# Scores of two steps behind the values, and PSUM banks handed out by hand, in top-k attention with a tanh-shrink feed-forward

## The chip, the cores and the metric

The kernel runs on one core of one Trainium2 chip. The metric is device microseconds (us), the median of the runs shown. A core has TensorE (PE in the profile; its weight loads are PEld), VectorE (DVE), ScalarE (ACT), GpSimd (POOL) and SyncE (SP, which here issues DMAs). [...]

## What is computed

```python
scores = scale * np.matmul(q, k.transpose(0, 1, 3, 2))          # (8, 8, 576, 576), head_dim 64
kth = np.partition(scores, -32, axis=-1)[..., -32:-31]
scores = np.where(scores >= kth, scores, -1000000000.0)
scores = scores - np.max(scores, axis=-1, keepdims=True)
attn = np.exp(scores)
attn = attn / (np.sum(attn, axis=-1, keepdims=True) + 1e-09)
x = np.matmul(attn, v)                                          # then (B,H,S,D) -> (4608, 512)
h = x @ w_in                                                    # 512 -> 2048
out = (h - np.tanh(h)) @ w_out                                  # 2048 -> 512
```

The two weight matrices come as 64-bit floats and are converted on the chip during the first steps; q, k and v are 32-bit floats.

## The kernel before, in words

The work is cut into 144 **steps**. A step is one tile of 128 query rows for a pair of heads (the two heads stand on partitions 0 to 63 and 64 to 127 of the operands); since 576 is 4 x 128 + 64, there are also remainder steps, which take the last 64 rows of two head pairs. Batch 0 has steps 0 to 17, every later batch 18 more. From batch 1 on, steps come in twos (two query tiles of one head pair), and the second of them is `last`.

A step passes through several stages, each some steps behind the one before. The loop over `n` (from -4 to 144 + LAG) issues, in this order, for its turn `n`:

- the mask of step n-1 (ACT L347, POOL L350) and the search of step n (DVE L297 to L319): the 32 largest scores of each row, in four rounds. Between rounds come small jobs: the reciprocal of step n-2 (DVE L389), its division (ACT L396) and its 32x32 transpose (DVE L427);
- the DMAs that spread the transposed weights over partitions (`spread_keys`, through a DRAM tile, into an `et` buffer);
- a share of the feed-forward work (`deal`);
- `values`, five steps (LAG) after a unit's last step: attention weights times v into a PSUM tile `av` (L492), then copied out by ACT (L512) into `xT`. Before step 45 (NEAR) this stands at the head of the turn instead;
- `scores(n+1)`: matmuls into the PSUM tile `scps` (L267), copied out by one ACT instruction (L275). DVE reads half of the scores from PSUM directly;
- the exponentials of step n-1 (ACT L370), more shares of `deal`, and loads (`todo`).

In batch 0 (`pe`) the transposes run on TensorE instead (L464, copied by ACT L467), with `values` two steps behind.

**The feed-forward part** works on units of 256 rows (or 128 for remainders). Its items are lists of matmuls: `ffn_h` fills a PSUM bank of 512 columns in two items (L543), after which ACT takes tanh (L555) and a copy (L556) out of it and POOL subtracts; `ffn_o` accumulates 16 matmuls of 512 columns in one bank (L564, in eight items), which ACT copies out (L574) for the store. How many items each `deal` issues is worked out from the stock and the due times of the units, so TensorE's order is fixed when the program is built.

[...] Each buffer of a pool is a tile of its own, and a new use of it waits for the readers of the old one. Every engine works its instructions in the order of issue; waits between engines are put in by the framework, which follows reads and writes of tiles.

Of the kernel before, what the change touches and what calls it, by code (L numbers as in the profile page):

```python
# [8 lines left out]
AF = mybir.ActivationFunctionType  # L9
# [11 lines left out]
LAG = 5  # L21

NEAR = 45


class Step:
# [25 lines left out]
def kernel(  # L52
# [47 lines left out]
    gpool = pool("g", 4)  # L100
    dpool = pool("d", 2, space=bass.MemoryType.DRAM)
    sc_ps = pool("sc_ps", 1, space=PS)
    zt_ps = pool("zt_ps", 2, space=PS)
    h_ps = pool("h_ps", 2, space=PS)

    ident = consts.tile([P, P], FP32, name="ident")
    make_identity(nc, ident[:])
# [32 lines left out]
    def convert(piece, slot):  # L140


        j, i = piece // CD, piece % CD
        if j < WJ:
            src, dst = moe_w_in[i * P : (i + 1) * P, j * NW : (j + 1) * NW], w_in[j][:, i, :]
        else:
            r0 = ((j - WJ) * FJ + i) * P
            src, dst = moe_w_out[r0 : r0 + P, :], w_out[j - WJ][:, i, :]
        raw, shifted, _ = slot
        nc.sync.dma_start(flat(raw), src.bitcast(U32))  # L150
        nc.sync.dma_start(
            flat(shifted).bitcast(U8)[:, 0 : 8 * NW - 4], src.bitcast(U8)[:, 3 : 8 * NW - 1]
        )
        yield
        hi = raw[:, :, 1]
        f = thpool.tile([P, NW], FP32, tag="th", name="f")
        fu = f[:].bitcast(U32)

        nc.vector.tensor_scalar(fu, hi, 20, 0x7FF, ALU.logical_shift_right, ALU.bitwise_and)  # L159

        e = h_ps.tile([P, NW], FP32, tag="h", name="e")[:] if j < WJ else f[:]
        nc.scalar.activation(e.bitcast(I32), fu, AF.Relu, bias=e896[:], scale=2.0**23)

        nc.vector.tensor_scalar(
            dst.bitcast(U32), shifted[:, :, 0], 0x0FFFFFFF, None, ALU.bitwise_and
        )
        nc.scalar.activation(dst, dst.bitcast(U32), AF.Copy, bias=1.0, scale=2.0**-28)
        yield

        nc.vector.scalar_tensor_tensor(  # L170
            out=fu, in0=hi, scalar=0x80000000, in1=e.bitcast(U32), op0=ALU.bitwise_and, op1=ALU.bitwise_or
        )
        nc.gpsimd.tensor_tensor(dst, dst, f[:], ALU.mult)
        yield
# [9 lines left out]
    def half(t):  # L184
        return slice(t * D, (t + 1) * D)
# [45 lines left out]
    def turn_rows(name, b, hp):  # L231

        d = kqpool.tile([P, S], FP32, tag=f"{name}T", name=f"{name}T")
        {"k": kT, "q": qT}[name][b, hp] = d
        x = raw.pop((name, b, hp))
        if not (b == 0 and hp and turned_pe[0]):
            nc.vector.transpose(d[:], x)  # L237
            return
        for c0, c1, w in ((0, J, P), (J, J + 1, R)):
            zt = zt_ps.tile([P, 512], FP32, tag="zt", name="zt")  # L240
            for c in range(c0, c1):
                o = (c - c0) * P
                nc.tensor.transpose(zt[:, o : o + w], x[0:w, c * P : (c + 1) * P], ident[0:w, 0:w])
            w = (c1 - c0 - 1) * P + w
            nc.scalar.copy(d[:, c0 * P : c0 * P + w], zt[:, 0:w])
# [9 lines left out]
    W2, W4 = S2 // NL, S4 // NL  # L255
    rest = consts.tile([P, 2, S4 + Q], FP32, name="rest")

    def scores(n):
        g = steps[n]
        ps = sc_ps.tile([P, 2, 2, 512], FP32, tag="sc", name="scps")  # L260
        for s in range(2):
            ks = slice(s * S2, (s + 1) * S2)
            for i in range(2 if g.rem else 1):
                qs = slice(JP, S) if g.rem else slice(g.qt * P, (g.qt + 1) * P)
                rows = half(i) if g.rem else slice(0, P)
                for t in range(2):
                    nc.tensor.matmul(  # L267
                        ps[rows, t, s, 0:S2],
                        qT[g.b, g.hp + i][half(t), qs],
                        kT[g.b, g.hp + i][half(t), ks],  # L270
                        start=True,
                        stop=True,
                    )
        sc = scpool.tile([P, 2, 2, S2], FP32, tag="sc", name="sc")
        nc.scalar.copy(sc[:], ps[:, :, :, 0:S2])  # L275
        st[n] = dict(sc=sc, ps=ps)

    def search(n, exact, between):

# [2 lines left out]


        x = st[n]
        sc, ps = x["sc"], x.pop("ps")
        m = x["m"] = mpool.tile([P, 2, TOP], FP32, tag="m", name="m")
        rounds = TOP // 8
        if exact:
# [3 lines left out]
            left = seen[1:]  # L292
        else:
            top = x["top"] = tpool.tile([P, 2, S4 + Q], FP32, tag="top", name="top")
            near, far = ps[:, :, 0, 0:S2], sc[:, :, 1, :]
            a, b = half_max, ps[:, :, 0, S2 : S2 + S4]
            nc.vector.tensor_tensor(b, near[:, :, S4:], far[:, :, S4:], ALU.max)  # L297
            nc.vector.tensor_tensor(a, near[:, :, 0:S4], far[:, :, 0:S4], ALU.max)  # L298

# [149 lines left out]
    def turn_pe(n):  # L449

        g, z = steps[n], st.pop(n)["z"]
        if g.rem:
            et = et_rem
        elif g.i:
            et = ets.pop(n - 1)
        else:
            et = et2[0]
        ets[n] = et
        et = tiles(et, g.nq)[:, :, :, g.i, :].rearrange("p a k j -> p k a j")
        for k0 in range(0, KC, J):  # L460
            kn = min(J, KC - k0)
            zt = zt_ps.tile([P, 512], FP32, tag="zt", name="zt")
            for k in range(kn):
                nc.tensor.transpose(  # L464
                    zt[:, k * P : (k + 1) * P], z[:, (k0 + k) * P : (k0 + k + 1) * P], ident[:]
                )
            nc.scalar.copy(  # L467
                et[:, k0 : k0 + kn],
                zt[:, 0 : kn * P].rearrange("p (k a j) -> p k a j", a=NG, j=G),
            )  # L470
            if k0:
                yield
# [2 lines left out]

        return x.rearrange("p (a i j) -> p i a j", a=NG, i=nq)

    def values(n):


        g = steps[n]
        nq, u = g.nq, g.unit
        et = tiles(ets.pop(n), nq)
        w = nq * P
        av = zt_ps.tile([P, 2, N], FP32, tag="zt", name="av")
        for i in range(2 if g.rem else 1):
            cols = half(i) if g.rem else slice(0, w)
            es = et[:, 2 * i : 2 * i + 2] if g.rem else et
# [1 line left out]
            for c in range(J + 1):  # L490
                for t in range(2):
# [4 lines left out]
                        start=(c == 0),  # L496
                        stop=(c == J),
                    )
        if g.pe:
            rx = rxs.pop(n)  # L500
            for i in range(nq):
# [31 lines left out]
    def ffn_h(u, item):  # L533
# [3 lines left out]
        for f in range(item * per, (item + 1) * per):  # L537
            j, fo = f // FJ, (f % FJ) * P
            s = f * w % 512
            if s == 0:  # L540
                cur[u] = h_ps.tile([P, 512], FP32, tag="h", name="hps")
            for c in range(CD):
                nc.tensor.matmul(  # L543
                    cur[u][:, s : s + w],
# [5 lines left out]
        if item % 2:  # L550
            th = thpool.tile([P, 512], FP32, tag="th", name="th")
            if item % 4 == 1:
                u.g.append(gpool.tile([P, 2, 512], FP32, tag="g", name="g"))
            g = u.g[-1][:, item % 4 // 2, :]
            nc.scalar.activation(th[:], cur[u][:], AF.Tanh)  # L555
            nc.scalar.copy(g, cur[u][:])  # L556
            nc.gpsimd.tensor_tensor(g, g, th[:], ALU.subtract)  # L557

    def ffn_o(u, i, part):
        if part == 0:  # L560
            cur[u] = h_ps.tile([P, DM], FP32, tag="h", name="ops")
        for f in range(2 * part, 2 * part + 2):
            o = f * u.n + i * P
            nc.tensor.matmul(  # L564
                cur[u][:],
                u.g[o // 1024][:, o % 1024 // 512, o % 512 : o % 512 + P],
                w_out[f // FJ][:, f % FJ, :],
                start=(f == 0),
# [2 lines left out]
        if part < CF // 2 - 1:  # L571
            return
        ot = thpool.tile([P, DM], FP32, tag="th", name="ot")
        nc.scalar.copy(ot[:], cur[u][:])  # L574
        for rows, dst in u.blocks[i]:
            nc.sync.dma_start(dst, ot[rows, :])

# [49 lines left out]
    def run(exact):  # L627
# [10 lines left out]
        for i, (b, hp) in enumerate(pairs):  # L638
            n = next(n for n, g in enumerate(steps) if (g.b, g.hp) == (b, hp))
            for x, name in enumerate("kq"):  # L640
                m = max(n - 5 + x, turned.get(name, -4))
                if b == 0 and not exact:
                    m = -4
                at(m, lambda x=(name, b, hp, exact): load_rows(*x))
# [4 lines left out]
                    at_round.setdefault((n - 1, 0), []).append(turn)  # L649
                    turned[name] = n - 1  # L650
                else:
                    at(n - 3 + x, turn)
                    turned[name] = n - 3 + x
            at(n + 1 if b else n - 1, lambda b=b, hp=hp: load_v(b, hp))


# [51 lines left out]


        ready, begun = {}, {}  # L710
        for m, g in enumerate(steps):
            if g.last:
                begun.setdefault(g.unit, m + g.lag)
                if m in done:
                    ready[g.unit] = m + g.lag + g.pe
        before, last = {}, {}
        for u in begun:
            k = 2 if u.tag == "xT" else 1
# [28 lines left out]
                credit -= 1  # L747
            credit = min(credit, 1.0)

        for n in range(-4, NS + LAG):  # L750
            pe = here(-2) and steps[n - 2].pe
            def due():
                for m in (n - LAG, n - LAG + 1, n - LAG + 2):
                    if 0 <= m < NS and steps[m].last and steps[m].lag == n - m:
                        values(m)

            if n < NEAR:
                due()
            share, usable = rate(), converted[0]
            if pe:  # L760
                w = turn_pe(n - 2)
# [11 lines left out]
                spread(n - 2)  # L773
            deal(0.0 if pe else 0.4)
            if n >= NEAR:
                due()
            if here(1):
                scores(n + 1)
            if pe:
                next(w)  # L780
            if here(-1):
# [16 lines left out]

    any_bad = xpool.tile([P, 1], FP32, tag="anybad", name="anybad")
    nc.vector.reduce_max(any_bad[:], bad[:].rearrange("p t n i -> p (t n i)"), axis=mybir.AxisListType.X)  # L800
    cnt = zt_ps.tile([P, 512], FP32, tag="zt", name="cnt")
    nc.tensor.matmul(cnt[0:1, 0:1], any_bad[:], ones[:], start=True, stop=True)
    flag = xpool.tile([1, 1], I32, tag="flag", name="flag")
    nc.vector.tensor_copy(flag[:], cnt[0:1, 0:1])
# [33 lines left out]
```

## Time and profile before

| | |
|---|---|
| runs | 1511.54 us median of 3 (1510.0 to 1512.67) |
| the profiled execution's own time | 1509.65 us |
| its span | 1507.5 us |
| mean granted TensorE clock | 0.982 |
| idle ahead of scores L267 | 18.4 us, of it 8.2 on the first qT, 6.7 on DVE L305 |
| ACT L370, L347, L396 | 288, 288 and 252 instructions of 0.77 us each |
| ACT L512 (values out) | 56 of 0.37 us, 28 of 0.22 us |
| DMA traffic | 221.68 MB, 147 GB/s |

The span is what the profiler saw of the program; the own time of the same execution also holds what lies around it. In a group's line, the columns are: source line, engine, operation, what it writes and reads, shapes, count; then busy time and mean ns of one; then the engine's idle time just before these instructions, and what ended it. A float32 matmul of the code shows as two records. Matmuls are pipelined, so a record's duration is longer than the distance to the next record; the distance is the price.

### The profile page before, as it was taken

Reading aid. Unit: us, or ns where it says so; the run is one execution under the profiler, and the core shown is the slowest. Engines: PE = TensorE matmul, PEld = TensorE weight load, DVE = VectorE, ACT = ScalarE, POOL = GpSimd, SP = SyncE. Lnnn points to the kernel's source line nnn. Section 1 sums busy time; section 2 is a strip of 40 time slices with the busy share of each in tenths; the row PEclk is TensorE's granted clock in tenths of the full one; section 3 lists DMA queues with packets and bytes.
Section 4 is the critical chain, followed back from the end, with each engine's and each line's share of the span. In section 5 each row is a group of like instructions: output and inputs, shape, how many; then the busy total and the mean of one; then the engine's idle time right before and its main releaser. Section 6 shows DMA issues by size and latency. Waiting matters only on the chain.

```text
span 1507.5 us, 25020 instructions
## 1 busy us (share of the span) xinstructions
PE 1426.5 (95%) x7332; PEld 908.2 (60%) x7332; DVE 1295.2 (86%) x4886; ACT 1004.9 (67%) x1813; POOL 879.1 (58%) x1370
## 2 busy tenths in 40 slices
PE   4667898999999999999999999999999999999998
PEld 2454656465666565656565665657575675656673
DVE  7999899999998999999989999899988989886100
ACT  4766777777776777777676676768676676766220
POOL 3777667566565575657565575747474664646120
PEclk9888999999999999999999999999999999999999
DMA  9954123657854685567655865466554766443400
GB/s 277 373 170 167 25 43 92 171 156 153 205 147 140 164 166 156 134 176 171 162 136 146 175 147 165 138 166 159 156 145 117 174 144 177 111 140 105 109 7 17
DMA packets 248563, 221.68 MB, mean 147 GB/s; under 512 B 190816, under 2 KB 197984, under 8 KB 241248
## 3 DMA queue, kind: packets, MB, share of 16 engines
q1 hardware_dynamic: 246640, 219.75, 56.0%
q8 instruction: 61, 1.00, 0.3%
q14 instruction: 86, 0.70, 0.2%
q10 hardware_dynamic: 1776, 0.22, 0.1%
HBM read 136.17 MB, written 83.76 MB: 146 GB/s over the span
## 4 chain that ended last, share of the span: by engine, by line
PE 74%; DVE 15%; ACT 4%; POOL 2%; DMA 2%; issue 1%; SPq 0%; ACTq 0%; DVEq 0%; POOLq 0%
PE ops L564 28%; PE hps L543 28%; PE av L492 9%; PE scps L267 8%; DVE m L316 3%; DVE top L309 2%; DVE rest L319 2%; DVE zx L427 2%; DVE ab L303 1%; DMA w_in<-in_k_dram 1%; DVE f L170 1%; PE zt L464 1%; DVE f L159 1%; DVE top L319 1%; DVE ab L298 1%
## 5 line engine op out<-in xcount | busy, mean ns | idle before, releaser
L564 PE MATMUL ops<-w_out,g 128*128 128x512 f32 x1152 | 517.5, 600 | 2.4 <-POOL bad L354 1.5
L543 PE MATMUL hps<-xT,w_in 128*128 128x256 f32 (+1 forms) x2176 | 466.7, 372 | 1.0 <-ACT g L556 0.9
L350 POOL TENSOR_TENSOR z<-sc,z 128x576 f32<-128x576 f32 x288 | 404.5, 1426 | 86.2 <-ACT z L347 86.2
L543 PEld LDWEIGHTS hps<-xT,w_in 128*128 128x128 f32 x2176 | 392.0, 192 | 75.8 <-issue 21.6
L564 PEld LDWEIGHTS ops<-w_out,g 128*128 128x128 f32 x1152 | 213.3, 191 | 262.3 <-issue 250.3
L347 ACT ACTIVATE z<-sc,tb 128x576 f32<-128x576 f32 x288 | 207.6, 769 | 141.9 <-POOL tb L334 141.2
L557 POOL TENSOR_TENSOR g<-g,th 128x512 f32<-128x512 f32 x144 | 183.6, 1277 | 145.7 <-ACT g L556 140.9
L396 ACT ACTIVATE z<-z,rd 128x576 f32<-128x576 f32 x252 | 180.7, 764 | 97.0 <-DVE rd L389 96.9
L370 ACT ACTIVATE z<-z,nb 128x576 f32<-128x576 f32 x288 | 221.6, 774 | 2.5 <-POOL z L350 2.4
L380 POOL TENSOR_SCALAR rd<-den 128x2 f32<-128x2 f32 x144 | 32.7, 227 | 312.9 <-ACT z L370 307.1
L267 PE MATMUL scps<-kT,qT 64*128 64x288 f32 (+1 forms) x1280 | 189.0, 447 | 18.4 <-DVE qT L237 8.2
L427 DVE STREAM_TRANSPOSE zx<-z 128x1152 f32<-128x1152 f32 x126 | 172.0, 1365 | 35.2 <-ACT z L396 34.6
L309 DVE MAX8 top<-ab 128x8 f32<-128x144 f32 x864 | 194.6, 295 | 0.0
L275 ACT COPY sc<-scps 128x1152 f32<-128x1152 f32 x144 | 160.4, 1114 | 41.8 <-PE scps L267 41.4
L316 DVE MAX8 m<-rest 128x8 f32<-128x168 f32 x576 | 161.6, 322 | 0.0
L267 PEld LDWEIGHTS scps<-kT,qT 64*128 64x128 f32 (+1 forms) x1280 | 102.4, 184 | 94.5 <-issue 19.9
L316 DVE MAX8 m<-top 128x8 f32<-128x144 f32 (+1 forms) x576 | 151.7, 305 | 0.0
L555 ACT ACTIVATE th<-hps 128x512 f32<-128x512 f32 x144 | 84.2, 585 | 64.5 <-PE hps L543 62.1
L303 DVE TENSOR_TENSOR ab<-scps,sc 128x576 f32<-128x576 f32 x144 | 107.6, 748 | 0.0
L297 DVE TENSOR_TENSOR scps<-scps,sc 128x288 f32<-128x288 f32 x144 | 64.6, 449 | 46.1 <-ACT sc L275 45.7
L354 POOL TENSOR_SCALAR bad<-top,tb 128x3 uint8<-128x3 f32 x288 | 95.0, 341 | 0.0
L492 PE MATMUL av<-et,vb 128*64 128x256 f32 (+1 forms) x640 | 76.8, 372 | 18.2 <-ACT et L467 18.2
(78 smaller groups left out, 1536.8 us busy)
## 6 DMA issues: line engine op xcount, KB each, us to landing
there<-zx SPq DMA_DIRECT2D x56, 1152.0 KB, 4.2
spare<-there SPq DMA_DIRECT2D x112, 288.0 KB, 4.7
et<-there SPq DMA_DIRECT2D x112, 288.0 KB, 5.2
kin<-in_k_dram SPq DMA_DIRECT2D x116, 72.0 KB, 2.9
vb<-in_v_dram SPq DMA_DIRECT2D x64, 128.0 KB, 5.9
out_dram<-ot SPq DMA_DIRECT2D x32, 256.0 KB, 3.3
qin<-in_q_dram SPq DMA_DIRECT2D x113, 72.0 KB, 3.7
there<-zx SPq DMA_DIRECT2D x14, 576.0 KB, 5.2
```

Of the source, the lines that this page charges most:

```text
L267: nc.tensor.matmul(ps[rows, t, s, 0:S2], qT[g.b, g.hp + i][half(t), qs], kT[g.b, g.hp + i][half(t), ks], start=True, stop=True,)
L309: nc.vector.max(top[:, t, o : o + 8], low[:, t, i, :])
L316: nc.vector.max(m[:, t, m8], seen[i][t])
L347: nc.scalar.activation(zv[:, t, :], scf[:, t, :], AF.Relu, bias=tb[:, t : t + 1], scale=-BIG)
L350: nc.gpsimd.tensor_tensor(zv[:, t, :], scf[:, t, :], zv[:, t, :], ALU.subtract)
L370: nc.scalar.activation(x["zv"][:, t, :], x["zv"][:, t, :], AF.Exp, bias=x["nb"][:, t : t + 1], scale=scale, accum_out=den[:, t : t + 1],)
L396: nc.scalar.activation(x, x, AF.Copy, scale=rds[n][:, g.i, t : t + 1])
L427: nc.vector.transpose(tiles(zx, g.nq)[:, :, :, g.i, :].rearrange("p c k j -> p k c j"), z[:].rearrange("p (k c j) -> p k c j", c=NG, j=G),)
L492: nc.tensor.matmul(av[half(t), 0, cols], vb[g.b, hp][:, t, c, :] if c < J else vr[g.b, hp][:, t, :], es[:, :, (J + 1) * t + c if c < J els ...
L543: nc.tensor.matmul(cur[u][:, s : s + w], w_in[j][:, c, fo : fo + P], u.xT[:, c, 0:w], start=(c == 0), stop=(c == CD - 1),)
L557: nc.gpsimd.tensor_tensor(g, g, th[:], ALU.subtract)
L564: nc.tensor.matmul(cur[u][:], u.g[o // 1024][:, o % 1024 // 512, o % 512 : o % 512 + P], w_out[f // FJ][:, f % FJ, :], start=(f == 0), sto ...
```

## The change

Four things, with new line numbers in parentheses.

- The pools `zt` and `h` have one buffer each, a tile of two banks (`zts`, `hbs`), and functions `zt_bank()` and `h_bank()` hand out the halves in turn. The feed-forward lines become L591 (for L543), L603, L604 (for L555, L556), L612 (for L564) and L622 (for L574); transposes are L495, their copies L498.
- From step 18 (PAIRS) on, `scores_of_two` makes the scores of steps n+1 and n+2 in one go, at every second turn: the first 320 columns of each head into `scps`, the last 256 into the two `zts` banks (L277), with two ACT copies for each step (L305, L306). The search reads its near half from `scps` as before (L328 to L336).
- `values` (L534, copied out by L560) no longer uses a `zt` buffer, but the half of `hbs` that the feed-forward part did not take last. It may hold two units' values side by side. Its turn is moved to the turns at which scores of two are made, so for every second unit one step later.
- Loads and transposes of k and q come one step earlier.

```diff
+PAIRS = 18
+WIDE = 320
...
-    zt_ps = pool("zt_ps", 2, space=PS)
-    h_ps = pool("h_ps", 2, space=PS)
+    zt_ps = pool("zt_ps", 1, space=PS)
+    h_ps = pool("h_ps", 1, space=PS)
+    zts = zt_ps.tile([P, 2, 512], FP32, name="zts")
+    hbs = h_ps.tile([P, 2, 512], FP32, name="hbs")
+    last_zt, last_hb = [0], [0]
+    def zt_bank():
+        last_zt[0] ^= 1
+        return zts[:, last_zt[0]]
+    def h_bank():
+        last_hb[0] ^= 1
+        return hbs[:, last_hb[0]]
...
+    def scores_of_two(n):
+        ps = sc_ps.tile([P, 2, 2, 512], FP32, tag="sc", name="scps")
+        ends = zts[:].rearrange("p t (i k) -> p i t k", i=2)[:, :, :, 0 : S - WIDE]
+        for i in range(2):
+            products(steps[n + i], lambda rows, t: ps[rows, i, t, 0:WIDE], slice(0, WIDE))
+            products(steps[n + i], lambda rows, t: ends[rows, i, t, :], slice(WIDE, S))
+        for i in range(2):
+            sc = scpool.tile([P, 2, 2, S2], FP32, tag="sc", name="sc")
+            scf = sc[:].rearrange("p t s k -> p t (s k)")
+            nc.scalar.copy(scf[:, :, 0:WIDE], ps[:, i, :, 0:WIDE])
+            nc.scalar.copy(scf[:, :, WIDE:S], ends[:, i])
+            st[n + i] = dict(sc=sc, near=ps[:, i])
...
-            near, far = ps[:, :, 0, 0:S2], sc[:, :, 1, :]
-            a, b = half_max, ps[:, :, 0, S2 : S2 + S4]
+            near, far = ps[:, :, 0:S2], sc[:, :, 1, :]
+            a, b = half_max, ps[:, :, WIDE : WIDE + S4]
...
-            zt = zt_ps.tile([P, 512], FP32, tag="zt", name="zt")
+            zt = zt_bank()
...
-    def values(n):
+    def values(*ns):
+        if steps[ns[0]].pe:
+            bank = zt_bank().rearrange("p (a n) -> p a n", a=2)
+            weigh(ns[0], bank)
+            put_values(ns[0], bank)
+            return
+        bank = hbs[:, last_hb[0] ^ 1].rearrange("p (a n) -> p a n", a=2)
+        for x, n in enumerate(ns):
+            weigh(n, bank[:, x:])
+        for x, n in enumerate(ns):
+            put_values(n, bank[:, x:])
...
-        av = zt_ps.tile([P, 2, N], FP32, tag="zt", name="av")
...
-                cur[u] = h_ps.tile([P, 512], FP32, tag="h", name="hps")
+                cur[u] = h_bank()
...
-            nc.scalar.activation(th[:], cur[u][:], AF.Tanh)
-            nc.scalar.copy(g, cur[u][:])
+            nc.scalar.activation(th[:], cur[u], AF.Tanh)
+            nc.scalar.copy(g, cur[u])
...
-            cur[u] = h_ps.tile([P, DM], FP32, tag="h", name="ops")
+            cur[u] = h_bank()
...
-                m = max(n - 5 + x, turned.get(name, -4))
+                m = max(n - 6 + x, turned.get(name, -4))
...
-                    at(n - 3 + x, turn)
-                    turned[name] = n - 3 + x
+                    at(n - 4 + x, turn)
+                    turned[name] = n - 4 + x
...
             if g.last:
-                begun.setdefault(g.unit, m + g.lag)
+                x = m + g.lag
+                if not g.pe:
+                    x += max(x - PAIRS, 0) % 2
+                    due.setdefault(x, []).append(m)
+                begun.setdefault(g.unit, x)
...
             if n >= NEAR:
-                due()
-            if here(1):
-                scores(n + 1)
+                of_step(n)
+            if here(1) and n + 1 not in st:
+                if n >= PAIRS and here(2):
+                    scores_of_two(n + 1)
+                else:
+                    scores(n + 1)
```

`products` holds the matmuls that stood in `scores`; `weigh` and `put_values` are the two halves of the old `values`, the matmuls and the copies.

More of the change, by code (lines that the diff above doesn't have):

```diff
@@ L159, in convert @@
         nc.vector.tensor_scalar(fu, hi, 20, 0x7FF, ALU.logical_shift_right, ALU.bitwise_and)
-        e = h_ps.tile([P, NW], FP32, tag="h", name="e")[:] if j < WJ else f[:]
+        e = h_bank() if j < WJ else f[:]
         nc.scalar.activation(e.bitcast(I32), fu, AF.Relu, bias=e896[:], scale=2.0**23)
@@ L256, with products @@
     rest = consts.tile([P, 2, S4 + Q], FP32, name="rest")
+    def products(g, out, ks):
+        for i in range(2 if g.rem else 1):
+            qs = slice(JP, S) if g.rem else slice(g.qt * P, (g.qt + 1) * P)
+            rows = half(i) if g.rem else slice(0, P)
+            for t in range(2):
+                nc.tensor.matmul(
+                    out(rows, t),
+                    qT[g.b, g.hp + i][half(t), qs],
+                    kT[g.b, g.hp + i][half(t), ks],
+                    start=True,
+                    stop=True,
+                )
     def scores(n):
-        g = steps[n]
         ps = sc_ps.tile([P, 2, 2, 512], FP32, tag="sc", name="scps")
@@ L262, in scores @@
             ks = slice(s * S2, (s + 1) * S2)
[L263 to L273, printed above, removed]
+            products(steps[n], lambda rows, t: ps[rows, t, s, 0:S2], ks)
         sc = scpool.tile([P, 2, 2, S2], FP32, tag="sc", name="sc")
         nc.scalar.copy(sc[:], ps[:, :, :, 0:S2])
-        st[n] = dict(sc=sc, ps=ps)
+        st[n] = dict(sc=sc, near=ps[:, :, 0, :])
+    def scores_of_two(n):
[10 more added lines that the diff above has]
+            st[n + i] = dict(sc=sc, near=ps[:, i])
     def search(n, exact, between):
         x = st[n]
-        sc, ps = x["sc"], x.pop("ps")
+        sc, ps = x["sc"], x.pop("near")
         m = x["m"] = mpool.tile([P, 2, TOP], FP32, tag="m", name="m")
@@ L461, in turn_pe @@
             kn = min(J, KC - k0)
-            zt = zt_ps.tile([P, 512], FP32, tag="zt", name="zt")
+            zt = zt_bank()
             for k in range(kn):
@@ L476, in in_order, with weigh @@
         return x.rearrange("p (a i j) -> p i a j", a=NG, i=nq)
-    def values(n):
+    def values(*ns):
[9 more added lines that the diff above has]
+            put_values(n, bank[:, x:])
+    def weigh(n, av):
         g = steps[n]
-        nq, u = g.nq, g.unit
+        nq = g.nq
         et = tiles(ets.pop(n), nq)
         w = nq * P
-        av = zt_ps.tile([P, 2, N], FP32, tag="zt", name="av")
         for i in range(2 if g.rem else 1):
@@ L498, in values, with put_values @@
                     )
+    def put_values(n, av):
+        g = steps[n]
+        nq, u = g.nq, g.unit
+        w = nq * P
         if g.pe:
@@ L564, in ffn_o @@
             nc.tensor.matmul(
-                cur[u][:],
+                cur[u],
                 u.g[o // 1024][:, o % 1024 // 512, o % 512 : o % 512 + P],
@@ L573, in ffn_o @@
         ot = thpool.tile([P, DM], FP32, tag="th", name="ot")
-        nc.scalar.copy(ot[:], cur[u][:])
+        nc.scalar.copy(ot[:], cur[u])
         for rows, dst in u.blocks[i]:
@@ L710, in run @@
         ready, begun = {}, {}
+        due = {}
         for m, g in enumerate(steps):
             if g.last:
-                begun.setdefault(g.unit, m + g.lag)
+                x = m + g.lag
[3 more added lines that the diff above has]
+                begun.setdefault(g.unit, x)
                 if m in done:
-                    ready[g.unit] = m + g.lag + g.pe
+                    ready[g.unit] = x + g.pe
         before, last = {}, {}
@@ L748, in deal, with of_step @@
             credit = min(credit, 1.0)
-        for n in range(-4, NS + LAG):
+        def of_step(n):
+            if n in due:
+                values(*due[n])
+        for n in range(-4, NS + LAG + 1):
             pe = here(-2) and steps[n - 2].pe
[L752 to L755, printed above, removed]
             if n < NEAR:
-                due()
+                of_step(n)
             share, usable = rate(), converted[0]
@@ L775, in run @@
             if n >= NEAR:
-                due()
-            if here(1):
-                scores(n + 1)
+                of_step(n)
+            if here(1) and n + 1 not in st:
[3 more added lines that the diff above has]
+                    scores(n + 1)
             if pe:
@@ L800 @@
     nc.vector.reduce_max(any_bad[:], bad[:].rearrange("p t n i -> p (t n i)"), axis=mybir.AxisListType.X)
-    cnt = zt_ps.tile([P, 512], FP32, tag="zt", name="cnt")
+    cnt = zt_bank()
     nc.tensor.matmul(cnt[0:1, 0:1], any_bad[:], ones[:], start=True, stop=True)
```

## The prediction

> **What bounds the kernel now.** I read the page first: engine shares, slices, chain of waits.
>
> ```profile
> span 1507.5 us, 25020 instructions
> ...
> PE 1426.5 (95%) x7332; PEld 908.2 (60%) x7332; DVE 1295.2 (86%) x4886; ACT 1004.9 (67%) x1813; POOL 879.1 (58%) x1370
> ...
> PE   4667898999999999999999999999999999999998
> ...
> PEclk9888999999999999999999999999999999999999
> ...
> PE 74%; DVE 15%; ACT 4%; POOL 2%; DMA 2%; issue 1%; SPq 0%; ACTq 0%; DVEq 0%; POOLq 0%
> ```
>
> TensorE is full from the sixth slice on, and the chain is its own. So the question about every edit is whether a matmul starts later. The groups by line say what it waited for:
>
> ```profile
> L564 PE MATMUL ops<-w_out,g 128*128 128x512 f32 x1152 | 517.5, 600 | 2.4 <-POOL bad L354 1.5
> L543 PE MATMUL hps<-xT,w_in 128*128 128x256 f32 (+1 forms) x2176 | 466.7, 372 | 1.0 <-ACT g L556 0.9
> ...
> L275 ACT COPY sc<-scps 128x1152 f32<-128x1152 f32 x144 | 160.4, 1114 | 41.8 <-PE scps L267 41.4
> ...
> L555 ACT ACTIVATE th<-hps 128x512 f32<-128x512 f32 x144 | 84.2, 585 | 64.5 <-PE hps L543 62.1
> ```
>
> The 144 tanh inputs (L543) and 36 outputs (L564) of the feed-forward part, 180 fillings of a PSUM bank, waited 3.4 us in all. The reason is in the code: a bank is emptied by ACT (tanh L555 and copy L556, or copy L574) while TensorE fills the other. Next, the timeline of TensorE in the middle, then ACT's and TensorE's in the tail, where ACT has little else to do:
>
> ```profile
> 707.69 1.95 PE L492 MATMUL av<-spare,vb 128*64 128x256 f32 x16
> 709.47 0.60 PE L492 MATMUL av<-spare,vr 128*64 128x256 f32 x4
> 710.00 1.24 PE L267 MATMUL scps<-kT,qT 64*128 64x288 f32 x8
> 711.17 7.13 PE L564 MATMUL ops<-w_out,g 128*128 128x512 f32 x16
> 718.24 1.24 PE L267 MATMUL scps<-kT,qT 64*128 64x288 f32 x8
> 719.41 2.84 PE L564 MATMUL ops<-w_out,g 128*128 128x512 f32 x6
> ```
>
> ```profile
> 1445.20 0.37 ACT L512 COPY xT<-av 128x256 f32<-128x256 f32 x1 [1.71 <-PE av L492]
> 1448.87 0.60 ACT L555 ACTIVATE th<-hps 128x512 f32<-128x512 f32 x1 [3.30 <-PE hps L543]
> 1449.37 0.58 ACT L556 COPY g<-hps 128x512 f32<-128x512 f32 x1
> ```
>
> ```profile
> 1445.05 13.22 PE L543 MATMUL hps<-xT,w_in 128*128 128x256 f32 x60
> ```
>
> Two prices come from here. Sixteen records of 512 columns take 7.13 us, 0.446 each, so 0.871 ns a column; 16 records of 256 fill a bank in 3.57 us. The bank begun at 1445.05 is full at 1448.62; its copy ends at 1449.95, 1.33 us later. TensorE does not see this today, being in the other bank.
>
> **Part 1: fewer score visits (a gain).** The eight score records of 710.00 are four pairs side by side: 8 x 288 x 0.871 / 2 = 1.00 us. The visit takes 1.17 (718.24 to 719.41), so entering and leaving cost 0.17. 62 pairs make 62 visits fewer: 62 x 0.17 = 10.5 us, all on TensorE. Bounds: nothing, to 25 us (0.4 a visit, the weight load's idle time at such a change being 0.38 to 0.76). Columns stay the same: 320 + 256 for 288 + 288.
>
> **Part 2: four score copies for two (ACT).** L275 takes 1.11 us for 1152 elements, copies of 512 take 0.58; a step's two parts (640 and 512) I put at 1.2, nearly nothing more. What changes is the lump: in the built program the first copy waits for a matmul of the second step, and DVE's first operation of the first step waits for the second step's first copy. So DVE starts about 4 us after the scores begin instead of 2.75 (710.00 to 712.75). DVE's 17.5 us a pair (1102.9 busy between 200 and 1376 us, 63 pairs) stay under the 18.7 that a pair takes now (the scores of step 18 start at 208 us, those of step 143 at 1376), and the second step's scores lie ready. I cost this at nothing while a pair takes TensorE over 20 us.
>
> **Part 3: the banks as one tile (the loss).** The two feed-forward banks become halves of one tile, hbs. In the built program, every wait named, the matmul that opens one half waits for the last ACT instruction that read the *other*: the one opening columns 512 on waits for the copy out of columns 0 to 511, which waits for the bank's last matmul, just issued. I counted TensorE's work between a filled bank and the matmul that waits for its emptying. Before: never under 3.57 us, hence the idle 1.0 and 2.4. After: none at all in 133 cases of L604 (tanh and copy) and 34 of L622 (output copy), of 180; 8 more have under 2.2 us. The values sit in the same tile and inherit the wait (25 of these cases). The overlap is gone: TensorE stops, ACT empties, TensorE goes on. All 7 us of feed-forward matmuls per step stand behind the waiting one, and the scores behind them.
>
> Price of a wait, lower end: 1.33 + 0.05 (a matmul starts 0.05 us after the ACT instruction that it waited for, as after L467) = 1.38; for the output copy 0.80. Upper end: I paired all L555/L556 with the bank's last matmul. Between 200 and 1376 us, bank end to copy end has a median of 2.42 and a mean of 2.59 us (1.11 when ACT is free), for L574 a mean of 2.04. But that queue stands since ACT there waits for DVE (L347 for tb 141 us, L396 for rd 97 us), and a slower TensorE lets DVE get ahead. So I follow one pair from the start of its scores. Scores done at 2.2, half a bank of feed-forward at 4.0. ACT: four score copies 2.0 to 4.3, exponentials (L370, two of 0.77 and 0.19) to 6.2, tanh and copy to 7.3: a stop of 3.3. In each of the next three banks ACT has two lots of 1.43 or 1.9 us against 3.57 of filling, and is waiting: 1.38 each. Mean 1.85. Where the bank is full before the values (12 pairs) the long stop is missing, about 1.45. I take 1.75, and 1.3 for the output copy.
>
> - Middle: 112 x 1.75 = 196 and 28 x 1.3 = 36.
> - Tail, ACT free: 14 x 1.38 + 5 x 0.80 = 23.
> - Opening (18 steps, 200 us): zts is one tile too, so the second bank of transposes waits for the first's copy, 0.59 and some 0.3 around it: 18 x 0.89 = 16; 13 waits on L554 of some 0.6 = 8; eight feed-forward banks = 11. TensorE is idle for 61 of these 200 us, so part is hidden: 20, bounds 0 and 40.
> - Values emptied behind the scores: the copy is 0.37 against 2.0 of scores; 5 for late ones, bounds 0 and 15.
>
> **Part 4: the clock.** The stretches of the opening show the price of a long stop (columns: time, PE, PEld, DVE, ACT, POOL busy, granted clock, DMA):
>
> ```profile
> 51.80:55.20 3.40, 0.01 (x2) 0.01 (x2) 3.40 (x12) 2.95 (x6) 3.25 (x5) 0.86 1.03 398
> 55.20:60.00 4.80, 3.48 (x17) 2.68 (x19) 4.77 (x18) 2.52 (x7) 3.83 (x8) 0.50 1.08 360
> ```
>
> After 3.4 us idle the clock is halved; the stops under 1.8 us elsewhere left it at 1.00, one of 2.4 us took 3.4 us of half clock. The long stop of 3.3 us comes in some 18 pairs; half of them at 3.4 us lost gives 30, bounds 0 and 70. [...]
>
> **Moved at no cost:** loads and turns of k and q come one step earlier, with the same distance between them and the same DMAs; values of every second unit one step later, still ahead of the reuse of their et buffer.
>
> [...]
>
> **Sum:** 196 + 36 + 23 + 20 + 5 + 30 - 10 = 300. On the profiled execution's 1509.65 us (span 1507.5 and 2.2 around it; the median of the runs is 1.9 higher) that is **1810 us**. All lower ends: 133 x 1.38 + 34 x 0.80 - 25 = 186, so 1696; all upper: 141 x 2.6 + 36 x 2.1 + 40 + 15 + 70 = 567, so 2077.
>
> **Rivals.**
> - *Faster, 1500.* The wait is met when TensorE arrives, and part 1 is left. For: as written, the code alternates the banks as before. It decides if some 1.4 us of other TensorE work lies between a full bank and the next opening; 167 of 180 have none. 6%.
> - *ACT free everywhere, 1700 to 1760.* Stops at their floor, no halved clock. For: DVE gains slack. Against: copies and exponentials stand ahead of the tanh after each pair. 20%.
> - *ACT's queue as it is today, 1880 to 2050.* Stops of 2.6 us, and the clock halved more often, which lengthens the stops' surroundings. For: today's mean. 26%.
> - *Forecast, 1760 to 1880:* 48%.
>
> Range 1700 to 1950: it leaves the first rival and the upper part of the third out. A measurement of this kernel tells 0.2% from no change; faster 0.05, within 0.2% 0.01, slower 0.94: the first rival's 6% and the rest.
>
> **What would show it.** Waits of L591, L612 and L534 on ACT's g and ot: some 170, together 200 to 300 us, in place of 3.4. TensorE's share near 80%, its busy sum near 1430. In the tail a gap of 1.3 to 1.4 us after every 3.57 us. DVE idle some 15% more, waiting on L305. Clock tenths of 9 with some 8s. Wrong if the waits on g are few, or if their mean is under 1.3 or over 2.2; if the clock holds, 30 go; if DVE's wait on L305 leads the chain, part 2 was not free.

## The result and the profile after

The changed kernel takes 1906.91 us (median of 4 runs, 1897.29 to 1912.35) against 1511.99: a ratio of 1.2608, 95% interval 1.2546 to 1.267. The profiled execution took 1901.9 us by its own time, its span is 1900.0.

The page after, first the shares and slices:

```profile
span 1900.0 us, 25054 instructions
...
PE 1505.7 (79%) x7332; PEld 944.6 (50%) x7332; DVE 1295.9 (68%) x4886; ACT 1022.8 (54%) x1937; POOL 878.1 (46%) x1370
...
PE   4667787778778888787878878787978878787887
...
PEclk7578998889999999999999999999999999999999
```

No engine is full any more. TensorE's digits, 9 from the sixth slice on before, are now mostly 7 and 8, and its busy sum rose by 79 us, for the same 7332 records: part of the time it ran at a lower clock (mean granted clock 0.935, before 0.982). What TensorE waited for (columns: engine and line, releaser, us in total, times, longest):

```profile
PE hbs L591 <- ACT g L604: 192.0, 105, 6.7
PE hbs L612 <- ACT ot L622: 28.6, 11, 5.6
PE hbs L534 <- ACT ot L622: 25.6, 13, 6.1
PE hbs L612 <- ACT g L604: 25.4, 16, 2.6
...
PE hbs L534 <- ACT g L604: 19.2, 12, 2.8
PE hbs L591 <- ACT ot L622: 17.9, 10, 4.4
```

These six rows are the wait on the other half of the tile: 167 times, 308.7 us, where the kernel before had 3.4 us. The other engines wait in turn; ACT's and DVE's rows:

```profile
ACT xT L560 <- PE hbs L534: 177.7, 51, 7.4
ACT th L603 <- PE hbs L591: 177.5, 69, 5.6
ACT z L378 <- POOL tb L365: 124.9, 95, 3.1
ACT z L427 <- DVE rd L420: 89.8, 60, 3.8
```

```profile
DVE scps L328 <- ACT sc L305: 250.8, 58, 7.7
DVE zx L458 <- ACT z L427: 134.7, 60, 7.5
```

TensorE and ACT now work by turns, and DVE, which waited 46 us for score copies, waits 251 for those of the pairs. ACT's own waits for DVE's chain (the mask for `tb`, the division L427 for the reciprocal) are only about a tenth smaller than before, when they were:

```profile
ACT z L347 <- POOL tb L334: 141.2, 116, 3.6
ACT z L396 <- DVE rd L389: 96.9, 62, 2.9
```

So DVE got no lead on ACT from a slower TensorE: it gets its scores from TensorE.

The three stages of the span (columns as in the prediction's stretches; the cuts are the scores of step 18 and of step 143):

```profile
0.00:243.50 243.50, 156.27 (x908) 106.71 (x908) 187.66 (x671) 142.38 (x266) 140.09 (x208) 0.77 0.51 160
243.50:1736.40 1492.90, 1214.64 (x5893) 755.92 (x5892) 1095.44 (x4177) 847.33 (x1609) 710.00 (x1130) 0.96 0.47 118
1736.40:1900.00 163.60, 134.77 (x536) 81.94 (x534) 12.80 (x39) 33.08 (x62) 28.02 (x32) 0.99 0.13 38
```

Before, the same stages took 208.3, 1167.4 and 131.8 us; they grew by 35, 325 and 32. The wait in its plain form stands at the end of the middle, where ACT has little else to do:

```profile
1718.87 3.72 PE L591 MATMUL hbs<-xT,w_in 128*128 128x256 f32 x16 [1.16 <-ACT g L604]
1723.76 3.72 PE L591 MATMUL hbs<-xT,w_in 128*128 128x256 f32 x16 [1.16 <-ACT g L604]
```

A bank of 3.57 us now comes every 4.89 us: 1.32 a wait, of which the profile shows 1.16 as idle. The rest counts as busy: the bank's 16 records last 3.72 us, 0.15 longer than the 3.57 after which a next matmul starts when none waits (from here on the drain).

**The account.** Span +392.5 us. TensorE's idle time went from 65.9 to 380.5: +315. By the clock's record TensorE was busy for 187.4 us at half clock, before for 38.7. But the record begins only at 19.6 us, in the kernel before at 50.9, and the profile counts what lies ahead of it as full speed. It was half: up to there the eight score records of a visit take 2.29 us in both kernels, as they do inside the changed kernel's recorded half-clock stretch from 23.0 to 98.1; at full clock they take 1.24 (710.00 in the prediction's timeline). One visit of the kernel before, ahead of its record, and one of the changed kernel, in that stretch:

```profile
47.92 2.29 PE L267 MATMUL scps<-kT,qT 64*128 64x288 f32 x8
```

```profile
26.84 2.29 PE L277 MATMUL scps<-kT,qT 64*128 64x288 f32 x8
```

With the busy time ahead of the record, 8.3 and 27.8 us, it is 195.7 against 66.5, and half of the difference is +65. Some 160 drains of 0.15: +24. A pair's scores take 2.14 us (1089.04 to 1091.18) where two visits took 2.34: 62 x 0.2 = -12. Sum 392. That it meets the span so closely may be partly chance: drains and visits are each one reading taken many times.

### The profile page after: what moved, and what is told of

Read it like the earlier page. It is cut to its first block, busy times and chain, and to the rows that moved or that the text cites. A ratio compares the mean times of both kernels' runs of the same rounds, so it can differ in the third digit from the quotient of the medians.

```text
span 1900.0 us, 25054 instructions
## 1 busy us (share of the span) xinstructions
PE 1505.7 (79%) x7332; PEld 944.6 (50%) x7332; DVE 1295.9 (68%) x4886; ACT 1022.8 (54%) x1937; POOL 878.1 (46%) x1370
## 3 DMA queue, kind: packets, MB, share of 16 engines
q1 hardware_dynamic: 246640, 219.75, 44.4%
## 5 line engine op out<-in xcount | busy, mean ns | idle before, releaser
L591 PE MATMUL hbs<-xT,w_in 128*128 128x256 f32 (+1 forms) x2176 | 515.8, 393 | 188.8 <-ACT g L604 172.3
L612 PE MATMUL hbs<-w_out,g 128*128 128x512 f32 x1152 | 523.3, 608 | 57.1 <-ACT ot L622 28.6
L591 PEld LDWEIGHTS hbs<-xT,w_in 128*128 128x128 f32 x2176 | 409.7, 203 | 295.6 <-ACT g L604 209.7
L612 PEld LDWEIGHTS hbs<-w_out,g 128*128 128x128 f32 x1152 | 217.3, 194 | 331.4 <-issue 256.7
L328 DVE TENSOR_TENSOR scps<-scps,sc 128x288 f32<-128x288 f32 x144 | 64.8, 450 | 280.6 <-ACT sc L305 250.8
L427 ACT ACTIVATE z<-z,rd 128x576 f32<-128x576 f32 x252 | 180.6, 764 | 90.7 <-DVE rd L420 89.8
L401 ACT ACTIVATE z<-z,nb 128x576 f32<-128x576 f32 x288 | 222.5, 782 | 4.4 <-POOL z L381 2.9
L603 ACT ACTIVATE th<-hbs 128x512 f32<-128x512 f32 x144 | 85.0, 590 | 181.6 <-PE hbs L591 177.5
L277 PE MATMUL scps<-kT,qT 64*128 64x320 f32 (+3 forms) x728 | 130.5, 487 | 8.3 <-DVE qT L251 8.0
L305 ACT COPY sc<-scps 128x640 f32<-128x640 f32 x124 | 86.9, 701 | 72.7 <-PE scps L277 71.6
L560 ACT COPY xT<-hbs 128x256 f32<-128x256 f32 x56 | 20.7, 370 | 177.7 <-PE hbs L534 177.7
L534 PE MATMUL hbs<-spare,vb 128*64 128x256 f32 (+1 forms) x896 | 77.9, 320 | 24.1 <-ACT ot L622 15.5
```

What stands on the lines that cost most here:

```text
L277: nc.tensor.matmul(out(rows, t), qT[g.b, g.hp + i][half(t), qs], kT[g.b, g.hp + i][half(t), ks], start=True, stop=True,)
L401: nc.scalar.activation(x["zv"][:, t, :], x["zv"][:, t, :], AF.Exp, bias=x["nb"][:, t : t + 1], scale=scale, accum_out=den[:, t : t + 1],)
L427: nc.scalar.activation(x, x, AF.Copy, scale=rds[n][:, g.i, t : t + 1])
L591: nc.tensor.matmul(cur[u][:, s : s + w], w_in[j][:, c, fo : fo + P], u.xT[:, c, 0:w], start=(c == 0), stop=(c == CD - 1),)
L612: nc.tensor.matmul(cur[u], u.g[o // 1024][:, o % 1024 // 512, o % 512 : o % 512 + P], w_out[f // FJ][:, f % FJ, :], start=(f == 0), stop=( ...
```

## The experiments

Ratios are to the kernel before, run on the same chip, with 95% intervals.

**One tile for the two feed-forward banks, and nothing else.**

```diff
-    h_ps = pool("h_ps", 2, space=PS)
+    h_ps = pool("h_ps", 1, space=PS)
+    hbs = h_ps.tile([P, 2, 512], FP32, name="hbs")
+    last_hb = [0]
+    def h_bank():
+        last_hb[0] ^= 1
+        return hbs[:, last_hb[0]]
...
-                cur[u] = h_ps.tile([P, 512], FP32, tag="h", name="hps")
+                cur[u] = h_bank()
```

> The kernel before with one edit: the two feed-forward banks are halves of one tile; scores one step at a time, values and transposes in their own buffers as before. Theory (the wait on the other half of the tile is the loss): of the 144 waits behind tanh and copy 107 have no TensorE work to cover them, 20 have under 2.2 us, and of 36 behind the output copy 21 have none. At the 1.83 us of idle time that the changed kernel shows for such a stop, and 0.16 of drain: 107 x 2.0 + 20 x 0.6 + 21 x 2.1 = 270, and some 20 to 40 for the halved clock: 1760 to 1820 us. Rival (the stops are long only because four score copies and two exponentials stand ahead of the tanh after a pair of scores): stops at their floor of 1.35 us, 107 x 1.35 + 21 x 0.8 = 160, no halved clock: 1660 to 1700 us. Second rival (one tile costs nothing, the pairs do): 1512 us.

Measured: 1782.31 us, 1.1794 (1.1776 to 1.1812). The theory's range; the two rivals are out. What TensorE waited for in this run:

```profile
PE hbs L550 <- ACT g L563: 172.6, 102, 6.8
PE hbs L571 <- ACT g L563: 24.1, 18, 1.9
PE hbs L550 <- ACT ot L581: 19.8, 11, 4.3
PE hbs L571 <- ACT ot L581: 18.5, 13, 5.4
```

One tile instead of two costs 271 us by itself, without pairs and with the values elsewhere. The stops are nearly as long as in the changed kernel (1.69 a wait in the first row, 1.83 there), so the score copies in a lump do not make most of their length.

**The control: the same function, two tiles.**

```diff
-    hbs = h_ps.tile([P, 2, 512], FP32, name="hbs")
+    hb = [h_ps.tile([P, 512], FP32, name=f"hb{i}") for i in range(2)]
...
-        return hbs[:, last_hb[0]]
+        return hb[last_hb[0]][:]
```

> The kernel before, with the feed-forward banks handed out in turn by a function, but as two tiles: the control for the run with one tile (1782 us). All theories: the waits are those of before, 1508 to 1515 us. Anything else would mean that handing out by hand costs something besides the wait.

Measured: 1509.94 us, 0.9991 (0.9981 to 1.0). Handing out by hand is free; the tile is what costs.

**The changed kernel with two feed-forward tiles** (the edit of the control, in the changed kernel).

> The changed kernel with the two feed-forward banks as two tiles, handed out in turn by the same function; all else as in the changed kernel, the two transpose banks still one tile. Theory: no wait without cover is left behind tanh or output copy; the 290 us of idle time, their drains and the halved clock of the middle go, the opening keeps its 35 us at most: 1500 to 1540 us. Rival (the score copies in a lump and DVE's late start are the loss): 1650 us or more.

Measured: 1615.17 us, 1.0687 (1.0671 to 1.0703). 292 us come back, so the shared tile is the main cause in the changed kernel too; but the theory's 1500 to 1540 is missed by 75 us, and its rival's 1650 as well. Another wait is there:

```profile
PE hb L534 <- ACT g L604: 44.9, 18, 4.3
PE zts L534 <- ACT et L498: 21.5, 8, 4.4
PE hb L534 <- ACT ot L622: 11.9, 5, 2.8
```

The values ask for the bank "not in use" when it has not been emptied yet: 57 us in 23 waits, 2.5 each. In the changed kernel this wait was part of the other: its two L534 rows have 44.8 us in 25 waits.

**The transpose banks as two tiles too.**

```diff
-    zts = zt_ps.tile([P, 2, 512], FP32, name="zts")
+    zb = [zt_ps.tile([P, 512], FP32, name=f"zb{i}") for i in range(2)]
...
-            nc.scalar.copy(scf[:, :, WIDE:S], ends[:, i])
+            for t in range(2):
+                nc.scalar.copy(scf[:, t, WIDE:S], ends[t][:, i])
```

> As the run before, and the two transpose banks are two tiles as well, so that the end columns of a step's scores take two ACT copies of 256 elements instead of one of 512 (six copies a pair instead of four). Theory: the opening's waits on the first bank's copy go, 15 to 35 us under the run before; what is left of the change is the saving at score visits, 10 us: 1495 to 1510 us. Rival (the opening's 35 us came from the halved clock or the feed-forward stops there, not from the transposes): within 5 us of the run before.

Measured: 1595.30 us, 1.0554 (1.0539 to 1.0568): 20 us less, as the theory has it; its absolute time fails with that of the run before. The scores of step 18 start at 210 us, where they started at 208 in the kernel before and at 228 in the run above.

**The two steps' scores as two tiles too.**

```diff
-        ps = sc_ps.tile([P, 2, 2, 512], FP32, tag="sc", name="scps")
+        ps = [sc_ps.tile([P, 2, 512], FP32, tag="sc", name="scps") for i in range(2)]
```

> As the run before, and the scores of the two steps of a pair lie in two tiles of two banks each, so that DVE's first operation waits for its own step's copies alone, and the first copy for its own step's matmuls. Theory (TensorE bounds a pair, DVE has slack): within 4 us of the run before. Rival (DVE's late start of 4 us a pair is on the path once the stops are gone): 15 to 60 us under it.

Measured: 1584.06 us, 1.0472 (1.0454 to 1.049): 11 us less. Between the two: DVE's late start is on the path, for little.

**The same tiles without pairs** (PAIRS = 1000, scores in one tile).

> All banks as tiles of their own, scores one step at a time throughout (PAIRS over the number of steps), values five steps behind as before, but in the feed-forward bank that was not taken last. Against the kernel with pairs and the same tiles (1595 us). Theory A (what was left after the split, some 80 us in the middle, is the values' wait for the idle bank to be emptied, 18 stops of 2.5 us and more, and the clock halved by them; pairs save 10): the values' wait stays, so 1575 to 1615 us. Theory B (what was left belongs to the pairs: copies in a lump ahead of the tanh, DVE starting late): 1512 to 1535 us.

Measured: 1555.99 us, 1.029 (1.0276 to 1.0304). It lies under theory A's range and over theory B's. Without pairs, the values in the feed-forward bank cost some 45 us: TensorE waits 25 us for the bank ahead of the values and 18 us ahead of feed-forward work for the values' copy out of it, where the kernel before had none of either. (Loads and transposes of k and q one step earlier are in this run too; the waits on them changed by under 1 us.) The pairs, meant to save 10, cost 39 more at this stage (1595.30 less 1555.99).

**No values while the bank in use is half full.** One more item is issued first, so that the other bank has had a whole filling to be emptied. On the kernel with all tiles split:

```diff
             if n >= NEAR:
+                if n in due and half_full[0] and work and work[0][0] <= usable:
+                    work.pop(0)[2]()
+                    credit -= 1
                 of_step(n)
```

> The run with all tiles split (scores too, 1584 us), and ahead of values one more feed-forward item is issued if the bank in use is half full, from step 45 on. The idle bank has then had a full filling (3.57 us) instead of half a one (1.78 us) to be emptied. Theory A: the 46 us of idle time on tanh and copy ahead of the values go, and most of the halved clock with them: 1515 to 1540 us. Theory B (DVE and the lump of copies bound the pair): the stops move to other places, 1570 us or more.

Measured: 1561.06 us, 1.0325 (1.0311 to 1.0339): 23 us less than without, where theory A had 44 to 69 and theory B 14 at most; neither range holds it. The row of the values' wait on tanh and copy shrinks from 46.0 us to 32.3 only.

**The same rule in the changed kernel.**

> The changed kernel, one tile for both banks, with the same rule: no values while the bank in use is half full, from step 45 on. Theory from the prediction's pair followed by hand (the long stop of some 3.3 us comes where the bank is half full at the values, because put-out copy, four score copies and two exponentials stand ahead of the tanh): those stops shrink to 1.5 us and the clock is halved less: 1840 to 1875 us. Rival (stops are long because ACT waits for DVE): within 1% of 1907 us.

Measured: 1932.39 us, 1.2771 (1.2751 to 1.2791). A miss: 25 us slower where 32 to 67 faster was expected; it lies outside the rival's 1% too. My reading of the long stops was wrong. This is what ACT did while TensorE stood still, between the scores of step 18 and those of step 143 (us):

| | changed | the rule | ACT's order, below |
|---|---|---|---|
| stops, sum | 278.1 | 292.9 | 223.2 |
| tanh, copy, output copy (the wait's own) | 130.3 | 130.9 | 135.0 |
| division (L427) | 51.4 | 61.7 | 10.6 |
| ACT idle | 35.4 | 44.4 | 15.0 |
| exponentials (L401) | 43.5 | 26.0 | 45.2 |

The rule did shorten the stops behind the exponentials, by 17 us; the division and idle time took 19 more. The changed kernel shows why, in ACT's timeline during one stop on an output copy:

```profile
1083.84 1.44 ACT L427 ACTIVATE z<-z,rd 128x576 f32<-128x576 f32 x2 [3.76 <-DVE rd L420]
1085.19 0.56 ACT L622 COPY ot<-hbs 128x512 f32<-128x512 f32 x1
```

The bank's last matmul ended at 1082.5. The copy that empties it starts 2.7 us later: it stands behind the division, and that had waited 3.76 us for DVE's reciprocal.

**DVE earlier, with the shared tile left in** (the score tiles split, in the changed kernel).

> The changed kernel, one tile for both feed-forward banks, with the scores of the two steps of a pair in two tiles, so that the first copy waits for its own step's matmuls and DVE for its own step's copies. Theory (the step of the prediction that failed is the one that cost DVE's late start at nothing: during the stops ACT spends 51 us in the division and 35 us idle, mostly waiting for DVE's reciprocal): DVE starts some 2 us a pair earlier, 62 pairs, and a third to two thirds of it comes off the stops: 1820 to 1870 us. Rival (DVE is in time, ACT's queue alone makes the stops long): 1890 to 1915 us.

Measured: 1884.64 us, 1.247 (1.2451 to 1.2489). 22 us less: outside both ranges, nearer to the rival. DVE's wait for the pairs' score copies shrank only from 251 to 214 us. It is TensorE that is late with the scores: of DVE's 243 us of waits for score copies in this run, 91 passed before TensorE had begun the scores and 104 while it made them.

**ACT's order alone.** From step 18 on, the first share of feed-forward work is issued ahead of the search, so that its tanh and copies precede the division; TensorE's order is untouched: its 7332 records come in the same order in both traces.

```diff
                 mask(n - 1, exact)
+            if n >= PAIRS and not pe:
+                deal(0.4)
...
-            deal(0.0 if pe else 0.4)
+            deal(0.0 if pe or n >= PAIRS else 0.4)
```

> The changed kernel with one change in ACT's order alone, from step 18 on: the first share of feed-forward work of a turn is issued ahead of the search, so tanh, copy and output copy of that share stand ahead of the division, which waits for DVE's reciprocal. TensorE's order stays the same. Theory (division and the wait for the reciprocal are 86 of the 278 us that TensorE stops in the middle): these go, and part of the halved clock: 1790 to 1840 us. Rival (the division is only moved: the next ACT instruction that TensorE or DVE needs comes as much later): 1880 us or more.

Measured: 1838.19 us, 1.217 (1.2151 to 1.2189): in the theory's range, the rival is out. The last column of the table is this run: division and idle time in the stops fall from 87 to 26 us.

**The same order with all tiles split and the full-bank rule.**

> All banks and scores in tiles of their own, no values while the bank in use is half full (1561 us), and ACT's order as in the run beside it. Theory: of the 68 us of stops left in the middle the division's 17, some idle time and the halved clock of these go: 1525 to 1545 us; under 1505 us only if all stops go, which would be the change's 10 us brought home. Rival: at 1555 us or more, the wait moves to DVE, whose transpose waits for the division.

Measured: 1522.58 us, 1.0077 (1.0064 to 1.0091): 38 us less than without the order, 2 us under the theory's range. Its page:

```profile
span 1520.7 us, 25181 instructions
...
PE 1411.6 (93%) x7332; PEld 919.6 (60%) x7332; DVE 1292.5 (85%) x4886; ACT 1024.8 (67%) x2081; POOL 878.8 (58%) x1370
```

TensorE's busy time is 15 us under that of the kernel before (1426.5), with more of it under a halved clock (52 us, before 39); at equal clocks it would be some 21. The score visits' 12 us are in it, and no run separates the rest. The idle time, 95.0 us for 65.9, and the clock eat it.

**NEAR at 18**, on top of that.

> The run with all tiles split, no values on a half-full bank and ACT's order changed (1523 us), with NEAR at 18 instead of 45, so that between steps 18 and 45 too the values stand right ahead of the scores and the full-bank rule holds. In that run 16 of the 30 stops left in the middle lie between 210 and 460 us (24 of 41 us), with 17 us of halved clock. Theory: most of these go, and the saving at score visits shows: 1495 to 1507 us, under the kernel before. Rival (the steps after batch 0 are bound by DVE, whose share there is 94%, and TensorE's stops there cost nothing): 1518 to 1524 us.

Measured: 1517.75 us, 1.0045 (1.0031 to 1.0058). The theory misses; it is the rival's time, within 0.3 us. In this run the values' wait on tanh and copy is nearly gone (13.8 us in the run before), and the scores wait for DVE instead (4.7 us in the run before):

```profile
PE scps L277 <- DVE top L338: 10.4, 4, 3.6
...
PE hb L536 <- ACT g L607: 2.8, 3, 2.0
```

From 210 to 460 us DVE is busy for 237 of 250, so a saving on TensorE can buy little there; that DVE is the only bound of this stretch isn't shown. No version here beats the kernel before. Whether pairs would, with a PSUM bank of their own for the values, wasn't tried; the kernel before takes eight banks, four for `scps`, two for `zt` (transposes and values) and two for `h` (feed-forward), and no kernel here takes a ninth.

## Why the prediction was right, and where it was not

The direction, the wait and the range held: 1906.91 lies between 1700 and 1950. The forecast itself, 1760 to 1880, did not: 1810 was 97 us short, and the time is that of the third rival (ACT's queue as it is today, the clock halved more often). The range held because it took in the lower part of that rival.

- **Part 3, the wait.** Right, shown by both sides: one tile in the kernel before costs 271 us, two tiles in the changed one give 292 back, and the same function with two tiles costs nothing. The count held: 167 waits foreseen with no cover, 167 in the six rows.
- **Its price where ACT is free.** 1.38 foreseen; 1.32 measured at the end of the middle, 1.38 in the tail (a bank every 4.95 us).
- **Its price behind tanh and copy in the middle.** 112 x 1.75 = 196 foreseen; 114 stops of 1.76 idle and 0.16 drain, some 218 us.
- **Its price behind the output copy.** 28 x 1.3 = 36 foreseen; 29 stops of 2.31 idle, 67 us. The copy stands behind a division that waits for DVE; with tanh and copies ahead of the division the 29 stops are 1.30 each.
- **"A slower TensorE lets DVE get ahead" (part 3), and part 2, "I cost this at nothing".** This step failed. ACT's waits for `tb` and the reciprocal went only from 141 and 97 us to 125 and 90, as DVE's wait for scores rose from 46 to 251. TensorE's pair was indeed longer than DVE's 17.5 us, but DVE sits between TensorE's scores and ACT's division, and ACT's division between TensorE and its bank. 87 us of the stops in the middle were division and idle time; moving tanh and copies ahead of the division takes 69 us off the kernel. The pairs make half of this share: counting only the stops on ACT's tanh, copies and output copies, it is 85 of 267 us here and 44 of 196 in the run with one tile and no pairs. DVE's wait on the second step's copy is the smaller part of this: 22 us.
- **The pair followed by hand.** The mean came out, the reason did not. It put the long stop on half-full banks and the exponentials; keeping values off half-full banks made the kernel slower. I had let ACT be waiting at each of the other banks; in fact its division was late there.
- **Part 4, the clock.** 30 foreseen, 65 by the account, 56 of it in the middle. The term was nine halvings at 3.4 us lost. A stretch of 3.41 us at half clock loses only half of that; but there were 31 halvings in the middle, 1.8 us each, as 40 stops were over 2.4 us and not 18. "After 3.4 us idle the clock is halved" was misread too: in the clock's record the halving comes at 54.28 us, 2.5 us into that stop. Nor was a stop of 3.4 us needed: in the changed kernel's middle 12 of the 20 stops of 2.4 to 3.0 us were followed by a halving. The busy sum, put near 1430, was 1505.7 for the most part by this term.
- **The opening and the tail.** 20 and 23 foreseen, 35 and 32 measured. The split of the transpose banks gives 20 back.
- **Part 1, the score visits.** 10.5 foreseen, 12 by the trace. Never seen as time: values and pairs together lose more.
- **What was not in the prediction.** The values' wait for the idle bank is a loss of its own, which the shared tile only hid; the half-full bank appeared there as a cause of a long stop and not as a price. It shows when the tile is split, and costs 45 us without pairs.

What stays open is how much of the pairs' 39 us is DVE's late start and how much the lump of copies: splitting the score tiles gave back 11, and no run separates the rest.

## What to carry to other kernels

Two buffers that are halves of one tile are one buffer to the framework that puts in the waits (one tile cost 271 us here, two tiles handed out by the same function nothing): look in the built program at which instruction the opening matmul waits for, and count the work between the two. "The bank not in use" was free here only where it had been emptied (57 us in 23 waits where it had not); price its emptying with everything that stands ahead of it on the emptying engine, and with what that waits for. When an engine that was hidden becomes part of the chain, the cheapest cure may be the order of its queue: here 69 us, without touching TensorE.

## What the runs showed of the hardware

The granted clock took two values, full and one half (39 stretches of each in the changed kernel's record, 9 of each in the kernel before's). Apart from a run's first and last, the stretches at one half lasted 3.41, 6.83 or 10.24 us; the first lasted up to 75.1 us (changed kernel). Whether a stop was followed by a halving (between its start and 4 us after its end), in the middles of all kernels here, the one before included:

| stop, us | stops | followed by a halving |
|---|---|---|
| 0.6 to 1.8 | 681 | 0 |
| 1.8 to 2.0 | 21 | 3 |
| 2.0 to 2.4 | 61 | 35 |
| 2.4 to 3.0 | 95 | 67 |
| over 3.0 | 112 | 104 |

In the changed kernel alone it is 0 of 108 up to 2.4 us, but only 3 of these were over 2.0; then 12 of 20, and 19 of 20. Over all kernels 38 of 82 stops of 1.8 to 2.4 us were followed by a halving. What one costs, in TensorE's timeline:

```profile
937.37 3.68 PE L534 MATMUL hbs<-spare,vb 128*64 128x256 f32 x16 [6.07 <-ACT ot L622]
```

After a stop of 6.07 us, 16 records that take 1.95 us in the kernel before took 3.68. This stop was paid twice, 6.07 us standing and 1.73 more running slowly.
